# Later casts for the second pair, one cast regrouped, a square moved to ScalarE, one more w_out block made ahead

## The chip, the cores and the metric

The kernel runs on one core of a Trainium2 chip. The metric is the device time of one execution in microseconds. TensorE (PE) multiplies, VectorE (DVE) and GpSimd (POOL) do elementwise work, ScalarE (ACT) does copies, casts and activation functions, and SyncE (SP) issues all the DMA transfers. Each engine works through its own instructions strictly in the order in which they are written, and waits at an instruction whose inputs another engine has not finished. The kernel before took 589.38 us (median of three runs, 588.06 to 589.50).

## The reference

Attention with a causal mask over 2 x 12 heads of 448 x 64, then two feed-forward blocks over 896 tokens of width 768:

```python
scores = where(mask, -1e9, q @ k.T / 8)               # per head, 448 x 448
x = softmax(scores) @ v                               # -> (896, 768)
h = x @ w_in                                          # 768 -> 2048
g = where(h >= 1, h, where(h <= -1, 0, (h + 1)**2 / 4))
x = g @ w_out                                         # 2048 -> 768
xn = x / sqrt(mean(x*x) + 1e-6) * rms_g
g, val = xn @ w_gate, xn @ w_val                      # 768 -> 1536
out = (g / (1 + exp(-g)) * val) @ w_out2              # 1536 -> 768
```

## The kernel before

Every operand of a matmul is split in two float32r parts, a high part (a cast by ScalarE) and a low part (value minus high part, by GpSimd or VectorE); a product of two operands is three matmuls (high x high, high x low, low x high). A matmul here is 128 x 128 by 128 x 448.

The weights come as 64-bit words. Three stage buffers take one block each (768 KB), and a block is made in steps that are written out by hand: `w_low` (the *low bits*, line 177, GpSimd, with a scaling by ScalarE in line 169), `w_high` (the *high words*, line 195, VectorE), and the split into parts (`parts`, lines 202 and 203, or the pair's own casts and subtractions). When a stage has been read, `w_next` issues the next load into it.

The products with w_in, and later with w_gate and w_val, use a scheme with seven products in place of eight for the two halves of the tokens and of the inner width. Two weight blocks make a *pair*; from a pair come four sums s1 to s4 (line 447) and with them up to seven operands. For pairs 2 to 7 of w_in the steps are those of `pair_steps`: `low`, `gate_high`, `val_high`, `sums_a`, `sums_b`, `hi` (casts, lines 477 and 478) and `lo` (subtractions, line 447 on VectorE and 482 on GpSimd). In `sums_a` stand a cast and a subtraction of the half block v2 (`parts`), and from pair 4 on the subtraction of the raw halves (line 468, whose cast is line 463). Pairs 0 and 1 have the steps of `early_steps`, whose last three, `split_a` to `split_c` (lines 536 and 537, and `parts`), are called by `early(NG, 3)` and `early(NG, 4)` for pair 1.

The products of w_in run in periods f = 0 to 7, one per pair. `p1` to `p7` are the products (line 649, nine matmuls each), `in1` to `in7` what is done with their results: bank copies by ScalarE (`in1` line 818, `in6` line 824, `in7` line 830), sums by VectorE (line 809), and an activation of relu (line 666), square (line 670 on ScalarE, 672 on GpSimd) and clip (line 675), which `later` puts off by one to three products. `preload_in` (line 812) copies a first result into the bank to which `p6` of the next period adds. Periods 1 to 3 are short, with five products each in the order 4 (of the pair before), 6, 3 (before), 7, 5; from period 4 on there are seven, and eight or nine at the end.

The loop over the periods has a list of products with a number behind each: `w_run(n)` then writes the next n weight steps, up to `w_cap`. `out1(0)` follows, the product with w_out for the first half of the tokens: 16 steps of 18 matmuls (line 952), each with an operand split by `gsplit` (cast line 887, subtraction line 888) and a w_out block made by `w_run(3)`: the split of one block, the high words of the next, the low bits of the one after that. The last two of the 16 steps are done together at the end.

## Time and profile before

| What | Value |
|---|---|
| median of three runs | 589.38 us (588.06 to 589.50) |
| the profiled execution | 588.19 us, of it the span of the instructions 586.5 us |
| TensorE busy | 568.8 us (97%), mean granted clock 0.996 |
| VectorE, ScalarE, GpSimd busy | 400.6 us (68%), 351.2 us (60%), 329.5 us (56%) |
| DMA | 71.35 MB, 122 GB/s over the span |

A matmul is pipelined: its own length is about 0.37 us, but the next one begins before it ends. "Idle before" is time in which an engine did nothing ahead of an instruction, and the name behind it is what released it. The granted clock is given as a share of full speed. Times on the axis of the trace count from the span's start; the products of w_in begin near 120 us in their periods, out1(0) at 215 us.

### The profile page before, as it was taken

What the parts mean: (1) busy time and instruction counts of PE and PEld (TensorE: products, weight loads), DVE (VectorE), ACT (ScalarE), POOL (GpSimd) and SP (SyncE); (2) the same over time, 40 slices, a digit from 0 to 9 for tenths busy, and PEclk for the clock granted to TensorE, in tenths of its full rate; (3) what the DMA queues carried; (4) which work ended last, traced back from release to release, by engine and by line L of the source; (5) the groups of instructions that cost most, each with busy time, mean ns of one, the idle gap of its engine ahead of it and who ended that gap; (6) DMA issues with size and microseconds to landing.
All of it is one profiled execution on the core that took longest, in us unless ns stands there. A gap on an engine that the chain in (4) does not pass through costs nothing.

```text
span 586.5 us, 8674 instructions
## 1 busy us (share of the span) xinstructions
PE 568.8 (97%) x3164; PEld 493.4 (84%) x3164; DVE 400.6 (68%) x666; ACT 351.2 (60%) x701; POOL 329.5 (56%) x256
## 2 busy tenths in 40 slices
PE   6999999989899999997999999999999999999997
PEld 3666667878789988986999998999999999999996
DVE  4777788768779777995558669766666656993110
ACT  4988988566667774555644567665555546544111
POOL 3465636755787678995656605575555554991000
PEclk9999999999999999998999999999999999999999
DMA  8344612134433335663353010435433334632002
GB/s 306 101 127 132 206 60 70 55 118 152 163 107 108 107 110 215 215 212 112 130 174 128 0 56 4 153 115 181 138 110 110 107 109 161 216 108 94 1 0 96
DMA packets 17851, 71.35 MB, mean 122 GB/s; under 512 B 2128, under 2 KB 6736, under 8 KB 17808
## 3 DMA queue, kind: packets, MB, share of 16 engines
q1 hardware_dynamic: 17808, 70.79, 35.7%
q8 instruction: 25, 0.41, 0.3%
q14 instruction: 18, 0.15, 0.1%
HBM read 68.03 MB, written 2.75 MB: 121 GB/s over the span
## 4 chain that ended last, share of the span: by engine, by line
PE 74%; DVE 11%; ACT 4%; issue 4%; POOL 4%; DMA 2%; SPq 1%; DVEq 0%; ACTq 0%; POOLq 0%
PE ps L649 33%; PE ps L1264 15%; PE ps L952 11%; PE ps L270 5%; PE ps L349 4%; PE ps L301 4%; DVE af L195 3%; DVE ar L888 2%; PE ps L335 2%; POOL af L177 1%; DMA af<-in_w_in 1%; DMA af<-in_w_out 1%; ACT af L169 1%; POOL ar L203 1%; DVE af L675 1%
## 5 line engine op out<-in xcount | busy, mean ns | idle before, releaser
L649 PE MATMUL ps<-ar 128*128 128x448 f32 x1260 | 260.3, 367 | 4.9 <-ACT af L830 2.9
L649 PEld LDWEIGHTS ps<-ar 128*128 128x128 f32 x1260 | 235.1, 188 | 28.5 <-ACT af L830 4.4
L203 POOL TENSOR_TENSOR ar<-af,ar 128x768 fp32r<-128x768 f32 (+1 forms) x56 | 94.6, 1690 | 66.9 <-ACT ar L202 56.7
L952 PE MATMUL ps<-ar 128*128 128x448 f32 x576 | 120.2, 370 | 3.3 <-ACT ar L887 1.7
L952 PEld LDWEIGHTS ps<-ar 128*128 128x128 f32 x576 | 108.9, 190 | 13.8 <-ACT ar L887 2.0
L195 DVE SCALAR_TENSOR_TENSOR af<-af 128x768 int32<-128x768 int32 (+1 forms) x78 | 101.9, 1308 | 20.3 <-POOL af L177 10.3
L177 POOL TENSOR_SCALAR af<-af 128x768 int32<-128x768 uint8 x76 | 88.5, 1164 | 6.9 <-DMA af<-in_w_out 0.8
L1264 PE MATMUL ps<-ar 128*128 128x448 f32 x432 | 87.9, 365 | 0.0
L1264 PEld LDWEIGHTS ps<-ar 128*128 128x128 f32 x432 | 81.1, 188 | 6.7 <-DVE ar L1211 0.3
L169 ACT ACTIVATE af<-af 128x768 f32<-128x768 f32 x73 | 65.7, 910 | 15.0 <-DMA af<-in_w_out 14.9
L202 ACT CAST ar<-af 128x768 fp32r<-128x768 f32 (+1 forms) x56 | 40.9, 730 | 35.7 <-DVE af L195 31.2
L285 ACT ACTIVATE af<-ps,nm 112x336 f32<-112x336 f32 (+2 forms) x96 | 47.3, 509 | 9.6 <-DVE nm L277 9.5
L1211 DVE TENSOR_TENSOR ar<-af,ar 128x448 fp32r<-128x448 f32 x24 | 29.2, 1226 | 32.3 <-ACT ar L1210 32.3
L888 DVE TENSOR_TENSOR ar<-af,ar 128x448 fp32r<-128x448 f32 x32 | 33.5, 1058 | 24.4 <-ACT ar L887 24.4
L277 DVE CUSTOM_DVE_ANT_0 ps<-ps,af 112x336 f32<-112x336 f32 (+2 forms) x96 | 41.4, 472 | 8.5 <-PE ps L270 7.4
L482 POOL TENSOR_TENSOR ar<-af,ar 128x768 fp32r<-128x768 f32 x18 | 33.7, 1875 | 21.6 <-ACT ar L478 21.6
L270 PE MATMUL ps<-af 64*112 64x448 f32 (+3 forms) x192 | 37.7, 450 | 5.6 <-DVE af L248 4.4
L1045 POOL TENSOR_TENSOR ar<-af,ar 128x448 fp32r<-128x448 f32 x15 | 18.1, 1218 | 30.6 <-ACT ar L1044 17.1
L270 PEld LDWEIGHTS ps<-af 64*112 64x112 f32 x192 | 17.6, 181 | 16.2 <-DVE af L248 4.4
L301 PE MATMUL ps<-ident,af 112*112 112x112 f32 x240 | 30.4, 266 | 0.0
L301 PEld LDWEIGHTS ps<-ident,af 112*112 112x112 f32 x240 | 22.9, 133 | 6.9 <-issue 3.3
L319 ACT COPY af<-ps 112x448 f32<-112x448 f32 x47 | 24.1, 544 | 7.3 <-PE ps L301 6.9
(108 smaller groups left out, 614.4 us busy)
## 6 DMA issues: line engine op xcount, KB each, us to landing
af<-in_w_out SPq DMA_DIRECT2D x28, 768.0 KB, 4.3
af<-in_w_in SPq DMA_DIRECT2D x20, 768.0 KB, 4.5
af<-in_w_gate SPq DMA_DIRECT2D x16, 768.0 KB, 4.7
af<-in_w_val SPq DMA_DIRECT2D x12, 768.0 KB, 4.3
af<-in_kT SPq DMA_DIRECT2D x12, 224.0 KB, 4.6
af<-in_qT SPq DMA_DIRECT2D x12, 224.0 KB, 4.9
af<-in_v SPq DMA_DIRECT2D x12, 224.0 KB, 2.9
out_T<-af SPq DMA_DIRECT2D x12, 224.0 KB, 1.9
```

The source lines that it names most:

```text
L169: nc.scalar.activation(c, c, ACTF.Prelu, scale=2.0 ** -112, alpha=-2.0 ** 32)
L177: nc.gpsimd.tensor_scalar(out=words(n, 0, I32), in0=b, scalar1=1.0 / 32, scalar2=-31.0 / 64, op0=ALU.mult, op1=ALU.add)
L195: nc.vector.scalar_tensor_tensor(out=out.bitcast(I32), in0=words(n, 1, I32)[:, c], scalar=3, in1=words(n, 0, I32)[:, c], op0=ALU.logical_s ...
L203: nc.gpsimd.tensor_tensor(out=lo, in0=src, in1=b32(hi), op=ALU.subtract)
L270: nc.tensor.matmul(bs[j][:C, o:o + (c + 1) * C], lhsT=q[r, c * C:(c + 1) * C], rhs=k[r, :(c + 1) * C], start=True, stop=True, skip_group_c ...
L277: nc.vector.tensor_tensor_reduce(out=t, in0=t, in1=mask[:C, S - (c + 1) * C:], scale=-1.0, scalar=3e38, op0=ALU.add, op1=ALU.min, accum_ou ...
L285: nc.scalar.activation(Pn[:C, j, poff[c]:poff[c] + w], sbank[n][j][:C, o:o + w], ACTF.Exp, bias=nm[:C, j, c:c + 1], scale=-1.0, accum_out= ...
L301: nc.tensor.transpose(bs[j][:C, o:o + C], Pn[:C, j, poff[c] + kc * C:poff[c] + (kc + 1) * C], ident[:C, :C])
L649: nc.tensor.matmul(b[:, :S], lhsT=w(a, k), rhs=x[:, c, k], start=first and k == 0 and i == 0, stop=(k == HK - 1 and i == 2), skip_group_ch ...
L888: nc.vector.tensor_tensor(out=t[:, 1], in0=G[h][:, kk], in1=b32(t[:, 0]), op=ALU.subtract)
L952: nc.tensor.matmul(ybs[dm][:, :S], lhsT=w[:, a, dm * P:(dm + 1) * P], rhs=t[:, c], start=(n == 0 and i == 0), stop=(n == NM - 1 and i == 2))
L1264: nc.tensor.matmul(obs[dm][:, :S], lhsT=w[:, a, dm * P:(dm + 1) * P], rhs=t[:, c], start=(kk == 0 and i == 0), stop=(kk == NF - 1 and i == 2))
```

## The change

Five edits. For pairs 2 to 4 the cast and subtraction of v2 move from `sums_a` to the end of `hi`. The three casts of pair 1 move behind the copies `in6(0)`, `preload_in(1)` and `in7(0)`, and the two weight steps that stood between them move behind `in5(0)`. The square of `in3` goes to ScalarE for f = 0 to 2. In periods 0 to 2 the cap reaches one pair further, so that the low bits of pairs 3 and 4 are written at the end of period 1 and 2 and not at the start of the next (six steps are written in period 1, seven in period 2). In the last period and behind it more steps are written, up to a fourth block of w_out, and in `out1(0)` two steps and not three at n = 10.

```diff
--- before.py
+++ after.py
@@ -463,7 +463,8 @@
                 nc.scalar.copy(bl[:, 0, 5:7], raw2)
 
         def sums_a():
-            parts(bl[:, 0, 4], bl[:, 1, 4], v2)
+            if not first or f > NA:
+                parts(bl[:, 0, 4], bl[:, 1, 4], v2)
             if f >= NA:
                 nc.gpsimd.tensor_tensor(out=bl[:, 1, 5:7], in0=raw2, in1=b32(bl[:, 0, 5:7]), op=ALU.subtract)
             tt(s1, v1, v2, ALU.add)
@@ -476,6 +477,8 @@
         def hi():
             nc.scalar.copy(bl[:, 0, 0:2], s12)
             nc.scalar.copy(bl[:, 0, 2:4], s34)
+            if first and f <= NA:
+                parts(bl[:, 0, 4], bl[:, 1, 4], v2)
 
         def lo():
             tt(bl[:, 1, 0:2], s12, b32(bl[:, 0, 0:2]), ALU.subtract)
@@ -795,7 +798,6 @@
     settle()
     early(NG, 2)
     tail_in(3)
-    early(NG, 3)
 
     if True:
         yb = [bank(f % 2) for f in range(NPR)]
@@ -868,7 +870,7 @@
         def in3(f):
             y, u = yb[f][:, :S], gm(1, f, 0)
             relu(u, y)
-            later(1, lambda: square(u, nc.gpsimd))
+            later(1, lambda: square(u, nc.gpsimd if f >= NA - 1 else nc.scalar))
             later(2, lambda: clip(u, u, y))
 
         IN = {1: (p1, in1), 2: (p2, in2), 3: (p3, in3), 4: (p4, in4), 5: (p5, in5), 6: (p6, in6), 7: (p7, in7)}
@@ -900,30 +902,30 @@
 
         for f in range(NPR):
             w_need(NA + 2 * f + 2)
-            w_cap[0] = NA + 2 * f + 4 if f < NPR - 1 else NW + 3
+            w_cap[0] = NA + 2 * f + (6 if f < NA - 1 else 4) if f < NPR - 1 else NW + 4
             if f == 0:
                 p6(0, range(HK - 1))
                 settle()
-                early(NG, 4)
                 p7(0, range(HK - 1))
                 p6(0, [HK - 1])
                 in6(0)
                 preload_in(1)
-                w_cap[0] = NA + 6
-                w_run(2)
+                early(NG, 3)
                 p7(0, [HK - 1])
                 in7(0)
+                early(NG, 4)
                 p5(0)
                 in5(0)
+                w_run(2)
                 continue
             if f < NA:
-                run = [(4, f - 1, 1), (6, f, 1), (3, f - 1, 2), (7, f, 1), (5, f, 2)]
+                run = [(4, f - 1, 1), (6, f, 1), (3, f - 1, 1 + (f > 1)), (7, f, 1), (5, f, 2)]
             elif f == NA:
                 run = [(p, f - (p in (3, 4)), 1) for p in (4, 1, 3, 6, 7, 5, 2)]
             elif f < NPR - 1:
                 run = [(p, f - (p in (3, 4)), 1) for p in (1, 4, 6, 3, 7, 5, 2)]
             else:
-                run = [(p, f - (p in (3, 4)), 1 + (p == 3)) for p in (4, 1, 3, 2, 6, 7, 5)]
+                run = [(p, f - (p in (3, 4)), 1 + (p in (3, 2, 5))) for p in (4, 1, 3, 2, 6, 7, 5)]
             for p, g, n in run:
                 IN[p][0](g)
                 IN[p][1](g)
@@ -936,7 +938,7 @@
             IN[p][0](NPR - 1)
             IN[p][1](NPR - 1)
             tick()
-            w_run(1)
+            w_run(1 + (p == 4))
         tick()
         w_cap[0] = NG2
         w_run(2)
@@ -956,7 +958,7 @@
                 presplit(h * NM + (min(n + 4, NM - 4) if h and n < 10 else n + 4))
                 if h == 0:
                     w_need(NW + n + 1)
-                    w_run(3)
+                    w_run(3 if n != NM - 6 else 2)
                 else:
                     early(n)
                 if n < NM - 2:
```

Below, lines 536 to 952 of the kernel before are lines 539 to 954 of the changed one; 202, 203, 169, 177 and 195 stay.

ScalarE at the start of the first period; L536 (L539) are the casts of pair 1, L824 (L826) and L830 (L832) the copies of in6(0) and in7(0), L812 (L814) the preload. Before:

```order
L536 CAST ar<-af 128x768 x2
L202 CAST ar<-af 128x384
L824 COPY af<-ps 128x448
L812 COPY ps<-af 128x448
L169 ACTIVATE af<-af 128x768 x2
L830 COPY af<-ps 128x448
```

and now:

```order
L826 COPY af<-ps 128x448
L814 COPY ps<-af 128x448
L539 CAST ar<-af 128x768
L832 COPY af<-ps 128x448
L539 CAST ar<-af 128x768
L202 CAST ar<-af 128x384
L169 ACTIVATE af<-af 128x768 x2
```

The three copies stand ahead of the casts, but for one cast, and the scaling of the next blocks (L169) stands behind all of them.

GpSimd in period 1, from the low bits of pair 2 (first row) to those of pair 3 (last rows); L203 and L482 (L485) are the subtractions of pair 2, L672 (L675) the squares. Before:

```order
L177 TENSOR_SCALAR af<-af 128x768 x2
L672 TENSOR_TENSOR af<-af 128x448
L203 TENSOR_TENSOR ar<-af,ar 128x384
L672 TENSOR_TENSOR af<-af 128x448
L482 TENSOR_TENSOR ar<-af,ar 128x768
L672 TENSOR_TENSOR af<-af 128x448
L177 TENSOR_SCALAR af<-af 128x768 x2
```

and now:

```order
L177 TENSOR_SCALAR af<-af 128x768 x2
L675 TENSOR_TENSOR af<-af 128x448
L203 TENSOR_TENSOR ar<-af,ar 128x384
L485 TENSOR_TENSOR ar<-af,ar 128x768
L177 TENSOR_SCALAR af<-af 128x768
L675 TENSOR_TENSOR af<-af 128x448
L177 TENSOR_SCALAR af<-af 128x768
```

One square is gone, the small subtraction stands directly ahead of the large one, and the last square stands between the two low-bit instructions.

ScalarE in the last period, from the scaling of w_out's second block on; L202 are casts of w_out blocks, L887 (L889) casts of out1 operands, L824 (L826) and L830 (L832) the copies of in6(7) and in7(7). Before:

```order
L169 ACTIVATE af<-af 128x768
L202 CAST ar<-af 128x768
L824 COPY af<-ps 128x448
L666 ACTIVATE af<-ps,half 128x448
L670 ACTIVATE af<-af 128x448
L887 CAST ar<-af 128x448 x2
L169 ACTIVATE af<-af 128x768
L830 COPY af<-ps 128x448
L887 CAST ar<-af 128x448
L202 CAST ar<-af 128x768
L666 ACTIVATE af<-af,half 128x448
L169 ACTIVATE af<-af 128x768
```

and now:

```order
L169 ACTIVATE af<-af 128x768
L202 CAST ar<-af 128x768
L169 ACTIVATE af<-af 128x768
L826 COPY af<-ps 128x448
L669 ACTIVATE af<-ps,half 128x448
L673 ACTIVATE af<-af 128x448
L889 CAST ar<-af 128x448 x2
L202 CAST ar<-af 128x768
L832 COPY af<-ps 128x448
L889 CAST ar<-af 128x448
L669 ACTIVATE af<-af,half 128x448
L169 ACTIVATE af<-af 128x768
```

The third block is scaled ahead of in6(7), the second block is cast ahead of in7(7), and the rows of the blocks after them follow correspondingly sooner.

## Rows read from the trace of the kernel before

**Rows 1.** Timeline of TensorE: start, length (us), line, operation, count [idle before].

```profile
124.85 2.09 PE L649 MATMUL ps<-ar 128*128 128x448 f32 x9 [1.17 <-ACT af L824]
...
127.33 9.39 PE L649 MATMUL ps<-ar 128*128 128x448 f32 x45 [0.39 <-ACT af L830]
...
137.71 11.76 PE L649 MATMUL ps<-ar 128*128 128x448 f32 x56 [0.99 <-ACT af L830]
...
149.79 7.29 PE L649 MATMUL ps<-ar 128*128 128x448 f32 x34 [0.32 <-DVE ar L447]
...
158.30 14.16 PE L649 MATMUL ps<-ar 128*128 128x448 f32 x65 [1.22 <-ACT af L830]
...
172.77 38.17 PE L649 MATMUL ps<-ar 128*128 128x448 f32 x187 [0.31 <-POOL ar L468]
...
269.42 0.47 PE L952 MATMUL ps<-ar 128*128 128x448 f32 x1 [1.68 <-ACT ar L887]
...
271.33 15.60 PE L952 MATMUL ps<-ar 128*128 128x448 f32 x68 [1.43 <-DVE ar L888]
```

**Rows 2.** Busy time by stretch, TensorE: length, busy (count), granted clock, DMA.

```profile
267.70:271.30 3.60, 0.52 (x2) 1.00 0.68 222
271.30:275.00 3.70, 3.67 (x10) 0.54 0.07 28
```

**Rows 3.** Timeline of ScalarE (ACT), 122 to 138 us.

```profile
122.31 1.63 ACT L536 CAST ar<-af 128x768 fp32r<-128x768 f32 x2 [0.69 <-DVE af L497]
...
124.28 0.52 ACT L824 COPY af<-ps 128x448 f32<-128x448 f32 x1
...
135.69 0.80 ACT L477 CAST ar<-ps 128x768 fp32r<-128x768 f32 x1 [1.79 <-DVE af L447]
...
136.39 0.83 ACT L478 CAST ar<-af 128x768 fp32r<-128x768 f32 x1
...
137.12 0.54 ACT L830 COPY af<-ps 128x448 f32<-128x448 f32 x1
```

**Rows 4.** Timeline of GpSimd (POOL), 123 to 173 us.

```profile
123.23 3.69 POOL L537 TENSOR_TENSOR ar<-af,ar 128x768 fp32r<-128x768 f32 x2 [9.04 <-ACT ar L536]
...
126.86 1.04 POOL L203 TENSOR_TENSOR ar<-af,ar 128x384 fp32r<-128x384 f32 x1
...
127.98 2.62 POOL L177 TENSOR_SCALAR af<-af 128x768 int32<-128x768 uint8 x2
...
137.30 1.84 POOL L482 TENSOR_TENSOR ar<-af,ar 128x768 fp32r<-128x768 f32 x1 [1.95 <-ACT ar L478]
...
139.10 0.94 POOL L672 TENSOR_TENSOR af<-af 128x448 f32<-128x448 f32 x1
...
140.12 2.11 POOL L177 TENSOR_SCALAR af<-af 128x768 int32<-128x768 uint8 x2
...
152.37 3.09 POOL L177 TENSOR_SCALAR af<-af 128x768 int32<-128x768 uint8 x2
...
164.40 3.08 POOL L177 TENSOR_SCALAR af<-af 128x768 int32<-128x768 uint8 x2
...
170.88 1.83 POOL L468 TENSOR_TENSOR ar<-af,ar 128x768 fp32r<-128x768 f32 x1
```

**Rows 5.** Timeline of VectorE (DVE), 135 to 160 us.

```profile
135.11 0.55 DVE L447 TENSOR_TENSOR af<-af,ps 128x384 f32<-128x384 f32 x1
...
144.23 0.57 DVE L195 SCALAR_TENSOR_TENSOR ps<-af 128x384 int32<-128x384 int32 x1 [0.24 <-ACT af L169]
...
147.35 0.56 DVE L447 TENSOR_TENSOR af<-af,ps 128x384 f32<-128x384 f32 x1
...
159.37 0.55 DVE L447 TENSOR_TENSOR af<-af,ps 128x384 f32<-128x384 f32 x1
```

**Rows 6.** Timeline of all engines, the end of out1(0).

```profile
265.44 2.60 DVE L195 SCALAR_TENSOR_TENSOR af<-af 128x768 int32<-128x768 int32 x1
...
268.81 1.96 ACT L887 CAST ar<-af 128x448 fp32r<-128x448 f32 x4
```

## The prediction, made before the changed kernel ran

> **What bounds the kernel now.** I read the waits of TensorE first, then its timeline, then the other engines where it waits. TensorE is busy for nearly the whole span, so a change can win only where it stands. Between 120 and 175 us it stands six times: 1.17 + 0.39 + 0.99 + 0.32 + 1.22 + 0.31 = 4.40 us [rows 1]. Near 269 us it stands 1.68 + 1.43 = 3.11 us [rows 1], and behind that its granted clock is 0.54 for 3.7 us [rows 2], which is a mean between the two levels, 2.4 and 1.2 GHz; 0.46 x 3.7 = 1.7 us of work is lost there. In the 3.6 us before the clock fell TensorE was busy for 0.52 us [rows 2]. So at most 4.4 + 3.1 + 1.7 = 9.2 us lie in reach.
>
> The stops before 175 us have two kinds. The first two are copies of a bank that stand late in ScalarE's queue: the copy before p5(0) starts at 124.28, behind two casts of pair 1 that began at 122.31 [rows 3]; TensorE waits 1.17 and then 0.39 us [rows 1]. The others come from a slower clockwork, the making of the pair blocks. It goes round through three engines: the low-bit instructions of pair k on GpSimd, high words and four sums on VectorE, casts on ScalarE, subtractions on GpSimd, and only then the low bits of pair k+1. I call the end of the fourth sum the *last sum*. It comes at 135.66 for pair 2, 147.91 for pair 3 and 159.92 for pair 4 (start plus length [rows 5]); the next low bits start at 140.12, 152.37 and 164.40 [rows 4], which is 4.46, 4.46 and 4.48 us later. A turn takes 12.25 and 12.01 us. A short period of TensorE is five products of nine matmuls; 45 of them take 9.39 us [rows 1]. So the clockwork is slower than TensorE up to pair 5, whose subtraction at 170.88 [rows 4] releases TensorE at 172.77 [rows 1]. After that no wait over 0.3 us comes until out1. **The time at which TensorE passes 172.77 is thus set by the clockwork and not by the copies.**
>
> **The change, part by part.** All times are those of the profiled execution: 588.19 us with a span of 586.5, inside the three runs (588.06 to 589.50) and 0.2% under their median.
>
> *Copies ahead of the casts.* TensorE ends p6(0) some 0.6 us before it runs dry at 123.68 (124.85 less 1.17 [rows 1]). The copy can then start near 123.15 and not at 124.28, and p5(0) starts 1.1 us sooner; the 0.39 before p4(0) goes too, since the second copy now follows one cast. Gain so far: 1.5 us. But the casts of pair 1 start after both first copies, at 124.0 and not at 122.31 [rows 3], so GpSimd's two subtractions start at 124.95 and not at 123.23 [rows 4]. Behind them on GpSimd are queued the 128x384 subtraction (1.04) and the low bits of pair 2, at 127.98 now [rows 4]; nothing in between is idle, so they start at 129.65. **The clockwork starts 1.6 us late.** Its cover was GpSimd's idle stretch before 123.23; now the delay is bare. Last sum of pair 2: 135.66 + 1.6 = 137.25.
>
> *One cast joins the others (pairs 2 to 4).* ScalarE's bank copy in7 no longer stands behind a cast that waits for the high words, so the 0.99 and 1.22 us [rows 1] lose their stated cause. The price is on GpSimd: its 128x384 subtraction waits for the joined cast, and the larger one and the next low bits are queued behind it. From the last sum on: casts 0.70 + 0.73 (starts at 135.69, 136.39, 137.12 [rows 3]) + 0.5 for the joined cast, estimated from the 0.73 of one with twice its columns, then 1.04 and 1.84 [rows 4] and small gaps, 4.95 us against 4.46 now. The square of in5 (0.94 [rows 4]) stood in those 4.46 and now stands between the two low-bit instructions. Turn 3 to 4 and turn 4 to 5 therefore grow by 0.49 + 0.94 = 1.4 us each. Turn 2 to 3 does not: the low bits ended at 142.23 and the high words started only at 144.23 [rows 4, 5], so 2.0 us of slack takes it up. VectorE's first sums of pair 4 meet the 1.84 us raw subtraction that now follows the low bits directly.
>
> *A square on ScalarE.* Three squares leave GpSimd (0.94 each [rows 4]). They stood where it waits for the sums anyway, so this gives nothing; on ScalarE they fall ahead of casts that wait too, so they cost nothing. If that cover were gone, at most 0.9 us per turn either way.
>
> *Low bits one period sooner.* In the program yes; on GpSimd they still stand behind the subtractions of the pair before, so they start when that is done. Taken as nothing beyond the above. ScalarE's copy into the bank of p6 now follows three casts: p6(2) would start at 139.7 (139.6 now: 137.71 and one product of 9.39 / 5 = 1.88 [rows 1]) and p6(3) near 151.5 to 152.5 (149.79 [rows 1]).
>
> Sum at p1(5): 1.6 + 0 + 1.4 + 1.4 = 4.4, with rounding 4.5 us late: about 177.3 and not 172.77. From p6(3) at 152 TensorE has eleven products of 1.88 to go, comes there at about 172.7 and stands over 4 us. *Bounds:* the two low-bit instructions take 2.11 us where VectorE leaves them alone, 3.09 and 3.08 in other turns [rows 4]. Were all as the quickest, two turns lose 2 us and the high words some 0.6 each: +1.3. Were all as the slowest and the raw subtraction in the way of the high words: +6.1.
> The Trainium skill, page "SBUF — State Buffer", section "SBUF: two separate sides", has a rule for this: GpSimd and a VectorE instruction with two SBUF inputs take one shared port pair by an exclusive lock, and the loser waits for the whole instruction. The 2.11 against 3.08 us [rows 4] fit it. By the rule alone the raw subtraction would hold pair 4's second high words for all of its 1.84 us, and the sum would be the upper bound; with no lock it would be the lower one.
>
> *A fourth out1 block.* Three more steps (one block's low bits, high words and split) are made in the last period of eight products, on engines that have idle time there, and one triple fewer stands in out1, whose VectorE runs without a gap. At its end the last high words (265.44, 2.60 us) and the cast behind them hold the last operand's cast until 268.81 [rows 6]; that is the 3.11 us. A triple done ahead is worth up to a turn, 3.75 us (two starts of the same group there, estimated from L195's 2.60 and a split). But each load waits for the stage that an earlier block's split frees, so I take a lead of about 2 us. Then 1 us of the 3.11 is left, and with no stop of 3 us the clock stays up: gain 2.1 + 1.7 = 3.8. Bounds 2.0 (half the lead, clock half lost) and 4.8 (all). The added casts in the last period sit ahead of in7(7); what they wait for is then done already, cost 0 to 0.3. The order on SyncE's queue stays; loads only follow their stages sooner.
>
> *Clock at p1(5).* A stop of 4 us is no shorter than the one that lowered the clock near 269 us [rows 1, 2]. That would cost 1.7, and nothing if it stays; I take half, 0.85.
>
> **Sum:** 588.19 + 4.5 - 3.8 + 0.85 = 589.7 us. A difference of 0.3% (1.8 us) is about what can be told from no change; this is within it.
>
> **Rivals.**
> *R1, the stops go and nothing comes instead (faster).* If the clockwork is not as closed as I read it, the 4.4 us go as well as 3.8 at out1: 580.0. If it only keeps today's pace, out1 alone counts: 584.4. For it: the cause named for four of the six stops, a late bank copy, is removed, and GpSimd loses three squares. Against: the wait before p6(3) and p1(5) is for the pair's parts themselves [rows 1], and their chain gets longer at two places. I set 583 for this case.
> *R2, the clockwork at its slowest (slower).* One mechanism, at p1(5): pair 5's raw subtraction ends 6.1 us later, at 178.9, because the raw subtraction of pair 4 gets in front of its high words; TensorE stands over 4 us and the clock falls: 588.19 + 6.1 + 1.7 - 3.8 = 592.2. It decides from a p1(5) later than 178 on. For it: low bits of 3.08 and 3.09 us in two of three turns [rows 4]. Against: three squares fewer to meet.
> *R3, the fourth block doesn't lead (slower).* If loads bound the first blocks, the late wait stays: 588.19 + 4.5 + 0.85 = 593.5. Against: VectorE is the one that is never idle there.
>
> **Chances.** My forecast (within 0.3%): 0.37. R1: 0.31, all faster. R2 0.23 and R3 0.09: slower, 0.32. So 0.31 faster, 0.37 same, 0.32 slower. The likeliest case's own range is 587.6 to 591.3 us. The range for 8 in 10 is 582.5 to 593.0: it leaves out R1's best and most of R3.
>
> **What would show it.** In the changed kernel's profile p5(0) starts near 123.8 with hardly a wait, and GpSimd's first low bits of pair 2 near 129.65. TensorE stands some 3 us before p6(2) (for the preload copy), 2 to 3.5 before p6(3), 3 to 4 before p1(5) (for GpSimd's raw subtraction), and passes there at 176 to 179. Late in out1 at most 1 us of waiting is left, and no stretch below full clock. I am wrong if p6(2) starts before 138.5, if p1(5) starts before 173, or if the wait at the end of out1 is still over 2 us.

## The result, and the profile after

The changed kernel takes 591.82 us (median of 9 runs, 591.39 to 594.53), the kernel before 589.50 beside it (9 runs, 586.89 to 590.12). The ratio is 1.0056 with a 95% interval of 1.0041 to 1.0071: slower by 0.56% over all runs; the two medians alone are 0.39% apart. The profiled execution of the changed kernel took 591.62 us with a span of 589.9, against 588.19 and 586.5.

The axes of two traces differ by a few tenths of a us before the periods begin. I put them on one another at the last group of matmuls of line 349, which no edit touches. It starts at 106.25 in the changed kernel (below) and at 106.51 in the kernel before. TensorE's timeline there, with the first matmul of out1 (line 952) and the sums of squares behind out1 (line 1016):

```profile
106.51 2.11 PE L349 MATMUL ps<-af 112*64 112x336 f32 x20
...
214.98 15.16 PE L952 MATMUL ps<-ar 128*128 128x448 f32 x74
...
286.77 0.85 PE L1016 MATMUL ps<-ones,af 128*112 128x1 f32 x8
```

So a time of the changed kernel plus 0.26 stands on the axis of the kernel before. "Late by" means after this shift.

TensorE's timeline in the changed kernel (start, length in us, line, count, [idle before and what released it]). Line 652 is 649 of before, 954 is 952, 1018 is 1016:

```profile
106.25 2.11 PE L349 MATMUL ps<-af 112*64 112x336 f32 x20
108.29 26.41 PE L652 MATMUL ps<-ar 128*128 128x448 f32 x126
136.25 2.09 PE L652 MATMUL ps<-ar 128*128 128x448 f32 x9 [1.55 <-ACT af L832]
139.44 9.75 PE L652 MATMUL ps<-ar 128*128 128x448 f32 x45 [1.09 <-ACT ps L814]
152.08 11.08 PE L652 MATMUL ps<-ar 128*128 128x448 f32 x45 [2.89 <-ACT ps L814]
164.46 7.57 PE L652 MATMUL ps<-ar 128*128 128x448 f32 x36 [1.30 <-DVE af L678]
173.39 4.31 PE L652 MATMUL ps<-ar 128*128 128x448 f32 x20 [1.37 <-ACT af L826]
178.09 38.16 PE L652 MATMUL ps<-ar 128*128 128x448 f32 x187 [0.39 <-POOL ar L469]
...
219.93 2.12 PE L652 MATMUL ps<-ar 128*128 128x448 f32 x9 [1.32 <-DVE af L811]
221.89 53.07 PE L954 MATMUL ps<-ar 128*128 128x448 f32 x256
275.99 14.04 PE L954 MATMUL ps<-ar 128*128 128x448 f32 x68 [1.03 <-DVE ar L890]
289.88 0.85 PE L1018 MATMUL ps<-ones,af 128*112 128x1 f32 x8
```

The two stops at p5(0) and p4(0) [rows 1] are gone: TensorE runs through from 108.29 to 134.70. Then it stands 1.55, 1.09, 2.89, 1.30, 1.37 and 0.39 us, 8.6 in all, where it stood 2.84 before from 137.71 on [rows 1]. p1(5) starts at 178.09, 5.58 us late against 172.77 [rows 1]. A new stop of 1.32 stands before p3(7), and out1 starts at 221.89, 7.17 late against 214.98. At the end of out1 one stop of 1.03 is left of 1.68 + 1.43 [rows 1]. The sums of squares behind it start at 289.88 against 286.77: 3.37 late. So out1 gives back 3.80 of the 7.17, and the 3.4 that remain are the whole difference of the spans. (1.4 of the 3.80 turn out below to be the clock's fall in this one profile of the kernel before.)

The granted clock (length, busy, clock, DMA share, GB/s). It falls behind the stop of 2.89 us, not at p1(5), and stays full at the end of out1, where it was 0.54 before [rows 2]:

```profile
152.00:156.00 4.00, 3.92 (x12) 0.57 0.00 0
176.00:180.00 4.00, 3.61 (x18) 1.00 0.48 178
276.00:280.00 4.00, 4.00 (x20) 1.00 0.04 14
```

The clockwork is seen at the first cast of a pair's sums, which follows the last sum within 0.05 us. ScalarE's timeline, pairs 2 to 5, with the copies for which TensorE stood at 136.25, 139.44 and 152.08 (line 832 is `in7`, 814 `preload_in`):

```profile
135.69 0.51 ACT L832 COPY af<-ps 128x448 f32<-128x448 f32 x1
137.01 0.80 ACT L478 CAST ar<-ps 128x768 fp32r<-128x768 f32 x1 [0.81 <-DVE af L447]
...
138.85 0.54 ACT L814 COPY ps<-af 128x448 f32<-128x448 f32 x1
...
149.65 0.80 ACT L478 CAST ar<-ps 128x768 fp32r<-128x768 f32 x1 [2.61 <-DVE af L447]
...
151.49 0.54 ACT L814 COPY ps<-af 128x448 f32<-128x448 f32 x1
...
163.90 0.80 ACT L478 CAST ar<-ps 128x768 fp32r<-128x768 f32 x1 [3.89 <-DVE af L447]
...
177.15 0.80 ACT L478 CAST ar<-ps 128x768 fp32r<-128x768 f32 x1 [1.58 <-DVE af L447]
```

Pair 2's cast stood at 135.69 before [rows 3]; 137.01 + 0.26 is 1.58 later. The turns are 12.64, 14.25 and 13.25 us. Those of the kernel before were 12.25, 12.01 and 11.88, from its casts at 135.69 [rows 3], 147.94 and 159.95 (0.03 behind the sums of [rows 5]) and this one:

```profile
171.83 0.80 ACT L477 CAST ar<-ps 128x768 fp32r<-128x768 f32 x1 [1.57 <-DVE af L447]
```

1.58 + 0.39 + 2.24 + 1.37 = 5.58, which is the delay of p1(5): **TensorE's loss there is the clockwork's, to the last tenth.**

The turn that grew most, on GpSimd and then on VectorE. Line 177 is the low bits, 675 a square, 469 the raw subtraction of pair 4, 195 the two halves of its second high words (the first half goes to ps, the second to af):

```profile
154.56 0.88 POOL L177 TENSOR_SCALAR af<-af 128x768 int32<-128x768 uint8 x1
155.53 1.71 POOL L675 TENSOR_TENSOR af<-af 128x448 f32<-128x448 f32 x1
157.32 1.32 POOL L177 TENSOR_SCALAR af<-af 128x768 int32<-128x768 uint8 x1
158.72 2.21 POOL L469 TENSOR_TENSOR ar<-af,ar 128x768 fp32r<-128x768 f32 x1
```

```profile
158.67 0.57 DVE L195 SCALAR_TENSOR_TENSOR ps<-af 128x384 int32<-128x384 int32 x1 [0.78 <-POOL af L177]
159.15 2.19 DVE L195 SCALAR_TENSOR_TENSOR af<-af 128x384 int32<-128x384 int32 x1
```

The raw subtraction starts at 158.72, the second half of the high words at 159.15, and this half takes 2.19 us. Elsewhere in the same trace the same instruction takes 0.55 when GpSimd is idle (at 146.54). In the kernel before a square stood in the subtraction's place, and the same half took 1.29:

```profile
155.55 1.31 POOL L672 TENSOR_TENSOR af<-af 128x448 f32<-128x448 f32 x1
```

```profile
155.97 1.29 DVE L195 SCALAR_TENSOR_TENSOR af<-af 128x384 int32<-128x384 int32 x1
```

And the new stop before p3(7), in the timeline of all engines (203 GpSimd's split of a w_out block, 890 VectorE's split of an operand, 195 the next block's high words, 811 the sum of in5(7)):

```profile
216.13 1.86 POOL L203 TENSOR_TENSOR ar<-af,ar 128x768 fp32r<-128x768 f32 x1 [0.96 <-ACT ar L202]
...
216.97 1.50 DVE L890 TENSOR_TENSOR ar<-af,ar 128x448 fp32r<-128x448 f32 x1 [0.27 <-ACT ar L889]
218.40 0.95 DVE L195 SCALAR_TENSOR_TENSOR af<-af 128x768 int32<-128x768 int32 x1
219.26 0.61 DVE L811 TENSOR_TENSOR af<-ps,af 128x448 f32<-128x448 f32 x1
```

The operand's split runs 1.50 us beside the block's split (0.61 for the one before it, at 215.56), the high words of the fourth block are next in VectorE's queue, and the sum for which TensorE waits until 219.93 stands behind both.

### The profile page after: what moved, and what is told of

It is laid out like the page before. It is cut to its first block, busy times and chain, and to the rows that moved or that the text cites. A ratio compares the mean times of both kernels' runs of the same rounds, so it can differ in the third digit from the quotient of the medians.

```text
span 589.9 us, 8677 instructions
## 1 busy us (share of the span) xinstructions
PE 569.4 (97%) x3164; PEld 493.8 (84%) x3164; DVE 396.9 (67%) x666; ACT 352.4 (60%) x704; POOL 326.7 (55%) x253
## 4 chain that ended last, share of the span: by engine, by line
PE 75%; DVE 8%; POOL 6%; issue 5%; ACT 2%; DMA 2%; SPq 1%; POOLq 0%; DVEq 0%; ACTq 0%
PE ps L652 35%; PE ps L1266 15%; PE ps L954 11%; PE ps L270 5%; PE ps L349 4%; PE ps L301 4%; DVE af L195 3%; DVE ar L890 2%; POOL af L177 2%; PE ps L335 2%; POOL ar L203 1%; DMA af<-in_w_in 1%; POOL ar L485 1%; POOL af L675 1%; DMA af<-in_w_out 1%
## 5 line engine op out<-in xcount | busy, mean ns | idle before, releaser
L203 POOL TENSOR_TENSOR ar<-af,ar 128x768 fp32r<-128x768 f32 (+1 forms) x56 | 95.2, 1701 | 78.2 <-ACT ar L202 67.9
L195 DVE SCALAR_TENSOR_TENSOR af<-af 128x768 int32<-128x768 int32 (+1 forms) x78 | 98.5, 1265 | 25.7 <-POOL af L177 16.5
L177 POOL TENSOR_SCALAR af<-af 128x768 int32<-128x768 uint8 x76 | 87.2, 1147 | 6.9 <-DMA af<-in_w_out 0.7
L169 ACT ACTIVATE af<-af 128x768 f32<-128x768 f32 x73 | 65.7, 909 | 16.9 <-DMA af<-in_w_out 16.9
L202 ACT CAST ar<-af 128x768 fp32r<-128x768 f32 (+1 forms) x56 | 40.9, 731 | 31.8 <-DVE af L195 27.1
L485 POOL TENSOR_TENSOR ar<-af,ar 128x768 fp32r<-128x768 f32 x18 | 33.7, 1874 | 16.4 <-ACT ar L479 16.4
```

Source lines behind the costliest of these rows:

```text
L169: nc.scalar.activation(c, c, ACTF.Prelu, scale=2.0 ** -112, alpha=-2.0 ** 32)
L177: nc.gpsimd.tensor_scalar(out=words(n, 0, I32), in0=b, scalar1=1.0 / 32, scalar2=-31.0 / 64, op0=ALU.mult, op1=ALU.add)
L195: nc.vector.scalar_tensor_tensor(out=out.bitcast(I32), in0=words(n, 1, I32)[:, c], scalar=3, in1=words(n, 0, I32)[:, c], op0=ALU.logical_s ...
L203: nc.gpsimd.tensor_tensor(out=lo, in0=src, in1=b32(hi), op=ALU.subtract)
```

## Experiments

Each kernel is an edit of the kernel before, of the changed one, or of the run named with it. In the table "first cast" is the start of pair 2's first cast of sums after the line-349 group, and "late" is that of pair 5's against the kernel before. Each row is one profiled execution. The same turns come back to 0.04 us in kernels that differ in other parts: the first and third row, and the second, fourth and fifth.

| Kernel | first cast | turns 2-3, 3-4, 4-5 | late |
|---|---|---|---|
| before | 29.18 | 12.25, 12.01, 11.88 | 0 |
| changed | 30.76 | 12.64, 14.25, 13.25 | +5.58 |
| out1 part alone | 29.18 | 12.24, 12.01, 11.88 | -0.01 |
| early parts without it | 30.57 | 12.64, 14.24, 13.25 | +5.38 |
| changed, copies put back | 29.17 | 12.63, 14.29, 13.26 | +4.03 |
| joined cast alone | 29.17 | 12.67, 13.38, 13.23 | +3.13 |
| low bits sooner alone | 29.17 | 11.99, 11.97, 11.87 | -0.32 |
| square alone | 29.19 | 12.25, 11.29, 11.89 | -0.70 |
| changed, raw subtraction behind | 30.70 | 12.63, 12.63, 15.36 | +6.00 |
| low bits first | 29.17 | 11.20, 11.40, 11.41 | -2.14 |
| both low bits first | 29.17 | 10.92, 9.93, 11.39 | -3.91 |
| the same, copies first | 30.70 | 12.44, 9.93, 11.39 | -0.86 |
| the same, chain started early | 28.88 | 10.93, 9.93, 11.38 | -4.20 |

### The out1 part alone

```diff
-w_cap[0] = NA + 2 * f + 4 if f < NPR - 1 else NW + 3   # kernel before
+w_cap[0] = NA + 2 * f + 4 if f < NPR - 1 else NW + 4
-run = [(p, f - (p in (3, 4)), 1 + (p == 3)) for p in (4, 1, 3, 2, 6, 7, 5)]
+run = [(p, f - (p in (3, 4)), 1 + (p in (3, 2, 5))) for p in (4, 1, 3, 2, 6, 7, 5)]
-            w_run(1)                              # behind p4(7), p3(7)
+            w_run(1 + (p == 4))
-                    w_run(3)                      # in out1(0)
+                    w_run(3 if n != NM - 6 else 2)
```

> The kernel before with the change's last part alone: one more weight step each behind p2(7), p5(7) and p4(7), one less in out1. Theory (the early parts lose 5.3 us up to p1(5), the last part gives out1 3.8 back, and the new wait of 1.3 us on the sum of in5(7) belongs to this last part, since the high words it queues in front of that sum wait for VectorE behind a GpSimd subtraction): p1(5) unmoved, the wait of 1.3 before p3(7) is there, the last matmul of out1 2.5 us earlier than in the kernel before, so about 585.7 on the profile's time and -0.42% against before. Rival (the wait before p3(7) comes from the early parts' delay, the weight stream being late against TensorE): no such wait, -3.8 us, -0.65%.

Measured: 587.56 us (12 runs) against 588.72, ratio 0.9984 (0.9964 to 1.0004). TensorE's timeline:

```profile
214.33 2.09 PE L649 MATMUL ps<-ar 128*128 128x448 f32 x9 [1.28 <-DVE af L809]
216.26 52.85 PE L952 MATMUL ps<-ar 128*128 128x448 f32 x256
```

The stop before p3(7) is there (1.28) with an early part that is the kernel before's: it belongs to this part. Out1 starts 1.56 late. From out1's start to the sums of squares it takes 67.92 us where the kernel before took 71.79. But the four other kernels with the old out1 (the early parts, and each of them alone) took 70.42, 70.75, 70.34 and 70.31, so 1.4 of the difference is not this part's. The run with the low bits sooner, below, shows what it is. What the part gives is 2.4 - 1.6 = 0.8 us, 0.14%, and not the 2.5 expected. That is what was measured (0.16%), though the interval of that still takes in no change.

### The sum of in5(7) first

```diff
-1 + (p in (3, 2, 5)))       # out1 part alone
+{3: 2, 5: 3}.get(p, 1))
```

> As the run before, but the extra step behind p2(7) is given two places later, behind in5(7), so that VectorE has the sum of in5(7) ahead of the high words. Theory (that sum is late only by what is queued ahead of it): no wait over 0.4 us before p3(7), and the fourth block still leads, -3.8 us, -0.65% against before, 1.3 us better than the run before. Rival (the fourth block needs the early step to be ready): the wait returns at the end of out1 with 1 us or more above the 1.0 of the changed kernel, and the two runs are equal within 0.3 us.

Measured: 587.26 us (12 runs), ratio 0.9984 (0.9964 to 1.0003), the same as the run before. TensorE's timeline:

```profile
213.16 3.92 PE L649 MATMUL ps<-ar 128*128 128x448 f32 x18 [0.21 <-ACT af L830]
...
228.54 43.43 PE L952 MATMUL ps<-ar 128*128 128x448 f32 x201 [0.19 <-DVE ar L888]
```

The stop is gone: p4(7) and p3(7) are one row, 18 matmuls. So the sum was late by what was queued ahead of it, as the theory says. But out1, from 216.91 to the sums of squares at 287.16, takes 70.25 us here and not 67.92, at full clock. Beside the stop at the end of out1 (1.28, in the run before 1.18) only one of 0.19 is listed. The rest are shorter ones, some 0.9 us of them near the row above: in each of the two stretches of 5 us from 226.9 on there are 24 matmuls, where 26 to 27 are usual. Most of the others come from 251 on, some 0.2 us more in each of six steps of 18 matmuls than in the run before. The rival has the outcome (the early step was needed, no gain), though the loss comes along out1 and not at its end.

### The early parts alone, and the changed kernel with the copies put back

The first is the changed kernel with the four edits above undone. The second undoes the first part:

```diff
     tail_in(3)
+    early(NG, 3)                   # changed kernel, copies put back
...
                 settle()
+                early(NG, 4)
                 p7(0, range(HK - 1))
                 p6(0, [HK - 1])
                 in6(0)
                 preload_in(1)
-                early(NG, 3)
+                w_run(2)
                 p7(0, [HK - 1])
                 in7(0)
-                early(NG, 4)
                 p5(0)
                 in5(0)
-                w_run(2)
```

> The changed kernel with its last part undone (steps in the last period and in out1 as before). Theory (the early parts alone lose 5.3 us by p1(5), nothing takes them back, and no wait before p3(7)): p1(5) at 178, out1's wait of 3.1 us back, +5.3 us, about 593.5 on the profile's time, +0.9% against before. Rival (the loss of the early parts is partly taken back further on because the weight stream gains slack against TensorE): the wait at the end of out1 shrinks below 2 us and the time is +3.5 us or less, +0.6%.

> The changed kernel with its first part undone: the casts of the first two pairs' last operand and pair 1's second half stand again ahead of the copies of in6(0), in7(0) and preload(1), the other parts stay. Theory (the clockwork of low bits, high words, sums, casts and subtractions starts 1.6 us late because of the first part, and each turn carries that on; the joined casts add 0.4 and 2.2 us to the turns): the last sum of pair 2 at 135.3 instead of 137.0, p1(5) at 175 to 176.5, about 2 us earlier than in the changed kernel, so the time 2 us below it, +0.2% against before at most. Rival 1 (the first part is the whole loss): p1(5) at 173, 5 us below the changed kernel, -0.35% against before. Rival 2 (the first part costs nothing, the joined cast and the low bits one period sooner do all): p1(5) at 177.5 or later, +0.5% against before.

Measured: the early parts 595.62 us (6 runs), ratio 1.0113 (1.0092 to 1.0134); copies put back 591.40 (7 runs), 1.0063 (1.0038 to 1.0089). The early parts lose 5.4 us at pair 5, have no stop before p3(7) and end slower than the whole change, as the theory says; its +0.9% is just under the interval. The 3.1 us of waiting at the end of out1 did not come back as such: one stop of 1.20 is listed there, the rival's sign. But out1 takes 70.42 us all the same, with some 0.3 us lost in nearly every step, and the rival's time is not met. With the copies put back the clockwork starts 1.59 earlier (29.17 against 30.76), on time, and the three turns are those of the changed kernel to 0.04 us. So the first part costs 1.55 us, once, and the other 4.03 come from the three other early parts. On the axis of the changed kernel the theory's p1(5) at 175 to 176.5 is 2.5 to 4.0 late and the second rival's 177.5 is 5.0, so 4.03 is at the theory's upper end. In time this kernel can't be told from the changed one.

### The joined cast, the low bits and the square, each alone

Each puts one part of the change into the kernel before:

```diff
-            parts(bl[:, 0, 4], bl[:, 1, 4], v2)        # joined cast, in sums_a
+            if not first or f > NA:
+                parts(bl[:, 0, 4], bl[:, 1, 4], v2)
...
+            if first and f <= NA:                      # in hi
+                parts(bl[:, 0, 4], bl[:, 1, 4], v2)
...
-w_cap[0] = NA + 2 * f + 4 if f < NPR - 1 else NW + 3   # low bits sooner
+w_cap[0] = NA + 2 * f + (6 if f < NA - 1 else 4) if f < NPR - 1 else NW + 3
-(3, f - 1, 2)
+(3, f - 1, 1 + (f > 1))
...
-square(u, nc.gpsimd)                                   # square
+square(u, nc.gpsimd if f >= NA - 1 else nc.scalar)
```

> The kernel before with one part alone: for pairs 2, 3 and 4 the cast of the last operand and GpSimd's subtraction behind it (1.0 us) come after the two casts of the sums, not before the sums. The turns, from one first cast of sums to the next, were 12.25, 12.01 and 11.88 us in the kernel before and 12.63, 14.29 and 13.26 in the run with the copies put back: 0.38, 2.28 and 1.38 more. Theory (this subtraction now stands in series between the casts and the next pair's low bits): all three turns grow by about 1.0 (the subtraction) less what its old place cost, 0.4 to 1.4 each, and this part alone gives 3 us or more of the 4.0 at p1(5). Rival (the low bits one period sooner, with the steps that they pull ahead, do it): turns within 0.3 of the kernel before's, p1(5) unmoved.

> The kernel before with one part alone: in periods 1 and 2 the cap on the weight steps is two items higher and one step fewer is given behind p3(0), so that every step of pairs 3 and 4 stands one place earlier. Theory (the joined cast makes the turns longer): turns as before within 0.3 us, and as the only effect the preload copies of p6(2) and p6(3) stand behind the casts of the sums, so waits of 1 to 3 us in front of these products, which the stops at p5 and p1(5) give back. Rival (this part makes the turns longer): 12.6, 14.3 and 13.3, p1(5) 4 us later than in the kernel before.

> The kernel before with one part alone: the squares of in3(0) to in3(2) on ScalarE. Theory (GpSimd's square stands off the path or 0.9 us in it, ScalarE's 0.6 stands before the copy of in6 and the casts): turns within 0.3 us of 12.25, 12.01 and 11.88, p1(5) within 0.5 of the kernel before's. Rival (it takes 0.9 us of GpSimd out of each turn): turns 0.9 shorter and p1(5) 1 to 2.5 us earlier.

One execution each, with a profile: 591.89, 586.97 and 586.22 us. The kernel before's 17 runs beside them spread from 586.72 to 594.18, so these times decide nothing; the turns are compared. ScalarE's first casts with the joined cast alone:

```profile
136.00 0.80 ACT L478 CAST ar<-ps 128x768 fp32r<-128x768 f32 x1 [1.83 <-DVE af L447]
...
148.67 0.80 ACT L478 CAST ar<-ps 128x768 fp32r<-128x768 f32 x1 [0.53 <-DVE af L447]
...
162.05 0.80 ACT L478 CAST ar<-ps 128x768 fp32r<-128x768 f32 x1 [3.96 <-DVE af L447]
...
175.28 0.80 ACT L478 CAST ar<-ps 128x768 fp32r<-128x768 f32 x1 [1.58 <-DVE af L447]
```

The joined cast gives 3.13 of the 5.58, with turns longer by 0.42, 1.37 and 1.35: the theory's range, and the forecast of 1.4 for the two later turns. TensorE loses more than that here: out1 starts 4.04 late (219.34), behind a stop of 1.75 and a granted clock of 0.63 over the 4 us after it. The low bits one period sooner cost nothing by themselves (-0.3), and bring a stop of 1.46 on a preload copy that doesn't delay pair 5. The square alone gains 0.70, all in turn 3 to 4: it leaves GpSimd where VectorE makes its second high words (0.55 us there, 1.29 in the kernel before). I had expected nothing over 0.3.

But the three add up to +2.1, and together they cost 4.03. Nearly all of the 1.9 between is in turn 3 to 4: added up it would be 12.01 + 1.37 - 0.04 - 0.72 = 12.62, and it is 14.29. The other two turns are those of the joined cast by itself (12.63 and 13.26 against 12.67 and 13.23). What the joined cast leaves on GpSimd beside and behind the second high words of pair 4 is a square (675) and then the raw subtraction (469):

```profile
157.65 1.30 POOL L675 TENSOR_TENSOR af<-af 128x448 f32<-128x448 f32 x1
158.91 2.14 POOL L469 TENSOR_TENSOR ar<-af,ar 128x768 fp32r<-128x768 f32 x1
```

The run with the low bits sooner answers the question from out1 too. Its out1 is the old one, with the old stops in front of the last operands:

```profile
269.80 0.47 PE L952 MATMUL ps<-ar 128*128 128x448 f32 x1 [1.67 <-ACT ar L887]
271.71 14.05 PE L952 MATMUL ps<-ar 128*128 128x448 f32 x68 [1.45 <-DVE ar L888]
```

```profile
268.00:271.70 3.70, 0.60 (x2) 1.00 0.70 226
271.70:275.70 4.00, 3.98 (x20) 1.00 0.04 17
```

1.67 + 1.45 us of stop with 0.60 us of work in 3.7, and the clock stays at 1.00; the kernel before's profile had 1.68 + 1.43 and 0.54 [rows 1, 2]. **The fall behind these stops comes in one execution and not in another.** The 13 to 24 timed runs of the kernel before beside the experiments have mean clocks from 0.991 to 1.000 too. A mean does not say where the clock fell, but one of 1.000 leaves no room for 1.7 us in 586 (0.003). So the 1.7 us that I booked as lost in the kernel before is lost only in some of its executions.

### The raw subtraction behind

```diff
-            if f >= NA:                             # changed kernel, sums_a
+            if f > NA or not first and f == NA:
                 nc.gpsimd.tensor_tensor(out=bl[:, 1, 5:7], in0=raw2, in1=b32(bl[:, 0, 5:7]), op=ALU.subtract)
...
         def lo():
+            if first and f == NA:
+                nc.gpsimd.tensor_tensor(out=bl[:, 1, 5:7], in0=raw2, in1=b32(bl[:, 0, 5:7]), op=ALU.subtract)
```

> The changed kernel, with GpSimd's subtraction of pair 4's raw gate words given with its other subtractions, behind the casts of the sums, not ahead of the sums. Together the joined cast and the low bits one period sooner make the turn from pair 3 to pair 4 14.25 us, where the joined cast alone makes it 13.38 and the other part alone 11.97; in the changed kernel the second high words of that turn take 2.19 us beside this subtraction. Theory (they stand behind it, VectorE and GpSimd being in one another's way, and the turn pays): these high words take 0.55 to 0.6, the turn falls by 1.6 to 12.6, and the next one grows by up to 1.85, since the subtraction now stands ahead of its low bits. Rival (the high words are long for another reason, or the turn waits for the square and the clip between them): the turn stays within 0.4 of 14.25.

Measured in one execution: 595.55 us. The second high words of pair 4, VectorE:

```profile
159.28 0.57 DVE L195 SCALAR_TENSOR_TENSOR ps<-af 128x384 int32<-128x384 int32 x1 [0.79 <-POOL af L177]
159.75 0.55 DVE L195 SCALAR_TENSOR_TENSOR af<-af 128x384 int32<-128x384 int32 x1
```

0.55 us in place of 2.19, and the turn 12.63 in place of 14.25: the theory to 0.05 us. The next turn grows by 2.11, more than the 1.85, and TensorE stands 3.62 us before the products of pair 4, with a granted clock of 0.50 over the 4 us behind that. 12.63 is also what the three parts give when they are added up (12.62). So what they do together beyond their sum is this one meeting. In the kernel before and with the joined cast alone a square stands beside these high words (1.29 us), and with the square alone moved to ScalarE nothing does (0.55). In the changed kernel the split of v2 (joined cast) and the square are both gone from between the low bits and the raw subtraction, which now comes directly behind the low bits and beside the high words (2.19). With the low bits sooner alone a square and the split of v2 still stand between (1.29 us). No run has two of the three parts; by the order of the rows above, the joined cast and the square would be enough.

### Low bits first, and what the first part is worth then

If the turn is one chain, taking something out of it must pay. In the first of these the step `low` of pairs 3, 4 and 5 is written ahead of `lo` of the pair before, on top of the run with the sum of in5(7) first; in the second the other low bits go ahead too, and the square of in3 goes to ScalarE:

```diff
-            steps.extend(w)         # the order of the steps of w_in
+            steps.extend(w[NA + 6 < n < NA + 13:-1] + (work[n + 2][:1] if NA + 4 < n < NA + 11 else []) + w[-1:])
-run = [(4, f - 1, 1), (6, f, 1), (3, f - 1, 2), (7, f, 1), (5, f, 2)]
+run = [(4, f - 1, 1), (6, f, 1), (3, f - 1, 1 + (f == 1)), (7, f, 1), (5, f, 2 + (f > 1))]
 # and in the second:
         def low():
-            w_low(n)                # False: without the scaling on ScalarE
+            w_low(n); w_low(n + 1, False) if first and 2 < f < 6 else None
         def gate_high():
...
-            w_low(n + 1)
+            w_scale(n + 1) if first and 2 < f < 6 else w_low(n + 1)
...
-            later(1, lambda: square(u, nc.gpsimd))
+            later(1, lambda: square(u, nc.gpsimd if f >= NA - 1 else nc.scalar))
```

> The kernel of the run with the sum of in5(7) first, and in the short periods the low bits of pairs 3, 4 and 5 are given to GpSimd ahead of the subtractions of the pair before, which wait for ScalarE's casts; the casts of the sums stay behind the preload copies. Theory (the turn is one chain: low bits, high words, sums, casts, subtractions, low bits, and TensorE's waits from p5(0) to p1(5) are paid by it): with the subtractions out of the chain the turns from one first cast to the next fall by 1 to 3 us, the stop at p1(4) of 1.35 and the one at p1(5) of 0.39 go, p1(5) comes 2 to 3.5 us earlier, and the time is 2 to 3 us under that of the run with the sum first, -0.6% to -0.8% against before. Rival (TensorE is the clockwork: the steps are given behind its products, and the low bits only wait longer for their high words): turns unmoved, p1(5) within 0.5 us of the kernel before's, the same time as the run with the sum first.

> The kernel of the run with the low bits first, with the second low bits of pairs 3, 4 and 5 ahead of the subtractions too, and the square of in3(0) to in3(2) on ScalarE as in the changed kernel. In the run with the low bits first the turns were 11.20, 11.40 and 11.41 us, and the second low bits still stood behind one subtraction of 1.85 and one square of 1.66. Theory (these two are the rest of the chain): turns of 10.2 to 10.8, p1(5) 1 to 2.5 us earlier than in that run, and -0.15% to -0.4% against it, -0.7% to -1.0% against before. Rival (five products of 2.0 us and TensorE's own stops set the turn by now): turns of 11.2 and more, the same time as that run within 0.1%.

Measured: 585.81 us (12 runs), ratio 0.9943 (0.9917 to 0.9969), and 583.54 (6 runs), ratio **0.9916 (0.9898 to 0.9933)**: both beat the kernel before, and with it the changed one. The second is in the expected range of time, the first at its edge. The second, TensorE's timeline:

```profile
138.09 70.38 PE L649 MATMUL ps<-ar 128*128 128x448 f32 x342 [0.98 <-ACT af L830]
...
212.50 11.45 PE L952 MATMUL ps<-ar 128*128 128x448 f32 x55
```

From 138.09 to 208.47 TensorE has no stop of 0.2 us or more; the kernel before had three stops there, 1.85 us. The turns of the first run fell by 1.05, 0.61 and 0.47, less than the 1 to 3 expected: it still had stops of 0.21 and 1.26, and out1 starts only 1.7 earlier than in the run with the sum of in5(7) first. In the second they are 10.92, 9.93 and 11.39, none of them in the 10.2 to 10.8 expected: TensorE sets the pace there. That the last one is longer because period 4 has seven products is likely, but no run shows it.

Then the first part of the change on top, and at last with the chain started early (the parts of the first part stay, two steps are moved):

```diff
                 settle()
+                w_cap[0] = NA + 6
+                w_run(1)            # low bits of pair 2
                 p7(0, range(HK - 1))
...
                 early(NG, 3)
+                w_run(1)            # its high words, the other low bits
                 p7(0, [HK - 1])
                 in7(0)
                 early(NG, 4)
                 p5(0)
                 in5(0)
-                w_cap[0] = NA + 6
-                w_run(2)
```

> The kernel of the run before, and the change's first part on top: the splits of the first two pairs' last operands behind the copies of in6(0), in7(0) and preload(1). Theory (this part takes 1.56 us of stops away from TensorE and starts the chain 1.58 later; it lost all of it because the chain was the limit): with the chain shortened to TensorE's own pace the stops taken away count, p1(5) 0.5 to 1.5 us earlier than in the run before. Rival (the chain is still the limit): the first casts of sums 1.58 later, each turn as in the run before, p1(5) 1.6 later.

> The kernel of the run with the copies first, and pair 2's low bits are given to GpSimd before pair 1's subtractions (the first of them ahead of p7(0), the second between the two subtractions), where GpSimd was idle for 10.7 us. Theory (the change's first part starts the chain late only because GpSimd does 3.7 us of pair 1's subtractions, and they wait for ScalarE's casts, ahead of pair 2's low bits; the chain decides when TensorE may go on): the first casts of pair 2's sums come 3 us or more earlier than in the run before, at the time of p3(0)'s end, the stop of 4.33 us shrinks below 1, and without the stops of 1.20, 0.39 and 0.98 out1 starts 2 to 2.6 us earlier than in the run with both low bits first; -0.3% to -0.45% against that run, -1.1% to -1.3% against before. Rival (pair 1's second half, now later on GpSimd, or pair 2's weights, not yet loaded, stop TensorE in their turn): a stop of 1 us or more in front of p7(1) or p6(2), and the time within 0.15% of that run or above it.

Measured: copies first 587.60 us (12 runs), ratio 0.9990 (0.9971 to 1.0008); chain started early 584.92 (8 runs), 0.9943 (0.9920 to 0.9965). One row of TensorE's timeline of each, and its clock around it, copies first and then started early:

```profile
139.14 71.91 PE L649 MATMUL ps<-ar 128*128 128x448 f32 x342 [4.33 <-ACT af L829]
```

```profile
139.10:143.10 4.00, 3.96 (x12) 0.59 0.00 2
```

```profile
137.60 70.39 PE L649 MATMUL ps<-ar 128*128 128x448 f32 x342 [1.93 <-ACT af L829]
```

```profile
137.60:141.60 4.00, 4.00 (x19) 1.00 0.00 0
```

My theory of a first part that pays once the turns are short fell. The stops at p5(0) and p4(0) go, and one stop of 4.33 takes their place: the copy of in7(1) is queued on ScalarE behind the first casts, and those wait for sums that are 1.53 late. The first turn is 1.52 longer as well (pair 5's cast comes 3.05 later, where the rival had 1.6), and in it TensorE's clock is 0.59 for 4 us, 1.6 us of work. With pair 2's low bits early the stop falls to 1.93 and the clock stays up. The first casts come 1.8 earlier, not 3: VectorE's high words end at 131.58 there and its first sum begins at 132.94, behind a square of GpSimd and a clip. Out1 then starts 105.30 us after the line-349 group, against 105.60 without the first part: 0.3 gained where 2 to 2.6 were expected. In time the two did not run beside one another, and the ratios overlap. On the traces the first part is worth next to nothing even when its harm is repaired.

## Why the prediction was right in its range and short in its size

The forecast was 589.7 us, the same within 0.3%; the measured 591.8 is slower by 0.56%, outside the likeliest case (587.6 to 591.3) and inside the range for 8 in 10. It is at the place and nearly the price of the second rival (592.2), and that price is met in part by luck: it held 1.7 for a clock that cost nothing there and nothing for the 1.6 before p3(7). Term by term, with the profiled executions:

- **Clockwork starts 1.6 late:** right. GpSimd's low bits of pair 2 start at 129.50 + 0.26 = 129.76 (129.65 forecast), the last sum ends at 137.24 (137.25), and putting the copies back takes 1.59 away.
- **Turns +0, +1.4, +1.4 from the joined cast:** right for what this cast does by itself (+0.42, +1.37, +1.35). From the last sum to the next low bits it is 4.95 us in the changed kernel, as forecast. The slack of 2.0 us in turn 2 to 3 took up all but 0.4: the square between the low bits took 1.70 there and not 0.94, beside VectorE's first high words, and the second high words waited for the low bits behind it (146.03). In turn 3 to 4 the square took 1.71, and the two low bits 0.88 + 1.32 and not 3.09: two sizes that were off and nearly cancel.
- **"2.11 us where VectorE leaves them alone":** misread. In that turn VectorE worked beside the low bits and was the one held up: a clip of 0.62 took 1.09 (at 140.38) and high words of 0.96 took 1.64 (at 141.39). In the turns of 3.09 and 3.08 VectorE's clip began first (152.32, 164.35) and GpSimd was held up.
- **The square and the low bits at nothing:** this is where most of the size went wrong. Alone they are nothing or a gain; together with the joined cast the raw subtraction of pair 4 falls on its second high words, 2.19 us in place of 1.29 beside the square and 0.55 when nothing is in the way. The forecast named this meeting ("VectorE's first sums of pair 4 meet the 1.84 us raw subtraction") and left it to the upper bound and to the second rival; it was the high words that it met, not the sums. Turn 3 to 4 grew by 2.24 and not 1.4, turn 2 to 3 by 0.39 and not 0: mis-sized by 1.1 us in all, 5.58 late and not 4.5.
- The rule of the Trainium skill, page "SBUF — State Buffer", section "SBUF: two separate sides" (an exclusive lock on the port pair that GpSimd and VectorE share, the loser waiting out the whole instruction), was the argument for that bound. The trace agrees: the subtraction runs from 158.72 to 160.93, the high words end at 161.34, 0.41 behind it, and moving the subtraction away gave 1.64 us back. The subtraction itself took 2.21 and not 1.85: it began 0.05 us behind the first half of the high words (158.67).
- **Where TensorE stands:** it stood 1.55 + 1.09 before p4(1) and p6(2) (some 3 forecast) and 2.89 before p6(3) (2 to 3.5 forecast). The stop before p4(1) was 0.99 and was to lose its cause. It came back as 1.55: the copy of in7(1) now stands on ScalarE behind a relu (134.54) that waited 1.29 us for VectorE's clip. Not 3 to 4 before p1(5): it came there late itself and stood 0.39, as three stops and the slow clock before it had used the time up.
- **Clock at p1(5), half of 1.7:** wrong place, and no cost. The clock fell behind the 2.89 us at p6(3). TensorE's lost work lies in time that it would have stood for the clockwork: p1(5) is late by the clockwork's 5.58 and nothing more.
- **"What they wait for is then done already, cost 0 to 0.3":** this step failed. I looked at ScalarE's casts in the last period and not at VectorE's queue. The extra high words (0.95) stand ahead of the sum of in5(7), behind an operand's split that takes 1.50 and not 0.63 with GpSimd's split of the block now beside it. The two cost 1.6 us; the out1 part alone shows it.
- **Fourth block 2.1 + 1.7 = 3.8:** the sum of 3.80 came to the digit, in part by luck. 2.4 us are the block's; 1.4 are the clock's fall in the kernel before's profile, which some other executions do not have.

1.1 + 1.6 more than forecast, less the 0.85 for the clock at p1(5), is 1.85, and the profiled execution came out at 591.62, 1.9 above 589.7. The first rival's faster case needed a looser clockwork; nothing here showed one. In the seven kernels (beside the one before) whose p1(5) has a row of its own it is late by what the clockwork is, to 0.02 us. With the joined cast alone and with the raw subtraction behind it has none: there TensorE was later than the clockwork, behind stops of 1.75 and 3.62 us and a slow clock. The third rival failed in the profile: the fourth block does lead.

## What to carry to other kernels

When a chain over several engines is slower than TensorE, price an edit by what it does to one turn of that chain, from the same event to its next occurrence; stops of TensorE that the edit removes come back at the next place where the chain is waited for. An edit that is free alone can change which instructions of two engines meet, so after adding up the parts look at what stands beside what on GpSimd and VectorE in the new order. When the chain is known, take something out of it: the kernel that gives the next pairs' low bits ahead of the subtractions that wait for casts, with the square on ScalarE and the fourth block, is 0.84% faster than the kernel before, where the five edits made it 0.56% slower.

## What the runs showed of the hardware that was not expected

- The same stops (1.68 + 1.43 and 1.67 + 1.45 us, half a us of work between them) were followed by a granted clock of 0.54 in one execution and 1.00 in another. After a stop of 2.89 and one of 4.33 us it was 0.57 and 0.59 over the next 4 us, after one of 1.93 it was 1.00, and yet after one of 1.75 (joined cast alone) it was 0.63.
- 128x384 high words with two SBUF inputs took 0.55 us alone, 1.29 beside a square on GpSimd and 2.19 beside a subtraction. The two GpSimd instructions lost time as well: 1.31 and 2.21 us, where they take 0.94 and 1.85 alone. In both cases the high words ended some 0.4 us behind them.
- A w_out block that is ready one step later cost TensorE 2.3 us (70.25 against 67.92 from out1's start to its sums of squares). The four later kernels with the same order in out1 took 69.13 to 70.03, so 1.2 to 2.3 in all. Nearly all of it is in stops of under 0.2 us that no row of the timeline lists: matmuls that begin 0.3 to 0.5 us after the one before and not 0.2.
